# Seven more warming matmuls behind the second product, and a fixed order for the first twelve products

## The chip, the cores and the metric

The kernel runs on one core of a Trainium2 chip. The metric is the device time of one execution in microseconds (us); less is better. The time of a kernel is the median over its runs. The profile is of one execution, and its times count from the first instruction of that execution.

## The reference

The inputs are 2048 tokens of 512 channels. Branch A is attention of 32 heads of 16 channels over a dilated local window (8 keys, every second token back). Branch B is a gated feed-forward layer with 1792 hidden channels. A sigmoid gate per token mixes both. Cut to what matters:

```
def _A_ref(x, wqkv, wo):
    qkv = (x @ wqkv) ...                      # 512 -> 3 * 512: queries, keys, values
    W, dil = 8, 2
    idx = pos[:, None] - (jnp.arange(W) * dil)[None, :]
    logits = where(idx >= 0, sum_d(q * k[idx]) * scale, -1e9)
    o = sum_w(softmax(logits) * v[idx])
    return o @ wo

def _B_ref(x, w_gate, w_up, w_down):
    return (gelu(x @ w_gate) * (x @ w_up)) @ w_down

g = sigmoid((x * gate_w).sum(-1, keepdims=True))
return g * _A_ref(x, ...) + (1 - g) * _B_ref(x, ...)
```

All of it is float32. All matrix products run on TensorE (PE); the local attention runs on VectorE (DVE).

## The kernel before, in words

Tokens are split by parity (even and odd), since the window has a step of two; each parity has 1024 tokens, in 8 tiles of 128 (`jj` from 0 to 7, two blocks `blk` of four tiles, `BT = 4`). The 512 input channels are four chunks `kc` of 128 (`KC = 4`). Every float32 operand is split into a high part in the type fp32r and a low part (the rest): `split` (L82 to L87) rounds on ScalarE (ACT, L86) or with a cast on DVE (L84), and DVE subtracts (L87). A product of two operands is then three matmuls: high by high, low by high, and high by low. In the text, a "product" is one such matmul of 128x128 by 128x512.

The kernel begins with `WARM = 31` matmuls of zeros in bfloat16 (L71, L72), 128x128 by 128x128 each, into a PSUM bank that nothing reads. They depend only on the memset of `warm` (L69). Behind them stand the products of the first stage: the keys and queries of half of the heads for the even tokens. For each chunk `kc` (loop at L795) the weights `WC[0, kc]` are loaded by `load_cb` (L164) and the tokens `X[0, blk, kc]` by the DMAs at L803; both are split. The very first token chunk (`kc = 0`, `blk = 0`) is loaded in two pieces of columns, the first 128 tokens (tile `jj = 0`) and the other 384 (tiles 1 to 3), so that the first products can begin before the second piece is there. The eight tiles accumulate in eight PSUM banks (`ps`, tags `p` and `acc0` to `acc3`; tile 7 has `acc3`), and `qkv_mm` (L185, matmul at L191) issues three products for each tile and chunk: 4 x 8 x 3 = 96 in the stage. In the profile the operands of chunk 0 and 1 show as `g` (weights), `A` (tokens of block 0) and `rt` (tokens of block 1).

Behind the first stage `take_first` (L196) copies the results out (ACT and DVE), then come the values (`project(0, 1)`), and the feed-forward layer `ffn` for the even tokens (products at L480 for gate and up, at L520 for down), into which the remaining projections are put as pieces; then the same for the odd tokens; last the output products (L742). The attention (`scores`, `softmax`, `mix`: long DVE instructions at L288, L291, L326, L330) is dealt out between these steps by `pull`.

The order on each engine isn't that of the text. A planner at build time plays the program through in simulated time and takes, on each engine, the instruction of the highest priority (place in the text, moved back by `BEHIND` for the attention) whose inputs are there at that simulated moment. `paced` (L347) adds an edge that only the planner sees: the instruction isn't planned ahead of the matmul that was recorded last in `LAST`. It costs no wait on the chip; each engine then runs its list in order, held by semaphores where data are needed.

Of the kernel before, what the change touches and what calls it, by code (L numbers as in the profile page):

```python
# [16 lines left out]
P = 128  # L17
# [11 lines left out]
UH = UC // DH  # L29
NU = D // UC  # L30
WARM = 31
BEHIND = 150
PACE = (0.9, 1.12)
LOAD = 4.0
BT = 4
# [9 lines left out]
def tile_gated_mix(ctx: ExitStack, tc: tile.TileContext, xt, wqkv, wff, wo, out):  # L45
    nc = tc.nc
# [17 lines left out]
    def bank(tag):  # L64
        return psum.tile([P, 512], F32, name=tag, bufs=BUFS.get(tag, 1))


    warm = pool.tile([P, P + 96], mybir.dt.bfloat16, name="warm")[:, :P]
    nc.vector.memset(warm, 0.0)  # L69
    idle = bank("p")  # L70
    for _ in range(WARM):  # L71
        nc.tensor.matmul(idle[:, :P], warm, warm, start=True, stop=True)  # L72
    zero = pool.tile([W, UC], F32, name="zero")
    nc.vector.memset(zero, 0.0)

# [23 lines left out]


    X, XOP, XR, WC = {}, {}, {}, {}
    LAST = []

    def fetch_x(par, kc):

# [79 lines left out]
    def qkv_mm(ps, par, jj, cb, kcs, c0=0, cn=512):  # L185
        t = slice((jj % BT) * P, (jj % BT + 1) * P)
        for kc in kcs:
            xh, xl = X[par, jj // BT, kc]
            wh, wl = WC[cb, kc]
            for n, (a, w) in enumerate(((xh, wh), (xl, wh), (xh, wl))):  # L190
                LAST[:] = [nc.tensor.matmul(ps[:, :cn], a[:, t], w[:, c0:c0 + cn], start=(kc == 0 and n == 0),  # L191
                                            stop=(kc == KC - 1 and n == 2))]
# [154 lines left out]
    def paced(ins):  # L347

        tc.add_manual_dep(ins.ins, LAST[-1].ins.name, mybir.DependencyInfo(mybir.DependencyClass.Sync,
                          mybir.DependencyReason.SCHED_ONLY), reason="pace")  # L350
# [39 lines left out]
    def pull(budget, key=None):  # L390
        credit[0] += budget
        while credit[0] > 0 and (key is None or key not in done):
            with tc.high_priority(offset=-BEHIND):
                c = next(fill, None)
# [80 lines left out]
    def product(ps, a, w, start):  # L475
        for kc in range(2):
            ah, al = XOP[a, kc]
            wh, wl = (x[:, kc * P:(kc + 1) * P] for x in w)
            for n, (w_, a_) in enumerate(((wh, ah), (wh, al), (wl, ah))):
                LAST[:] = [nc.tensor.matmul(ps, w_, a_, start=(start and kc == 0 and n == 0),  # L480
                                            stop=(kc == 1 and n == 2), skip_group_check=True)]
# [27 lines left out]
    def down(par, gr, t, b):  # L509
# [6 lines left out]
        for i in range(2):  # L516
            hh_, hl_ = Hs[2 * gr + i, b]
            d = WD[2 * gr + i]
            for n, (a, w) in enumerate(((hh_, d[:, :512]), (hh_, d[:, 512:]), (hl_, d[:, :512]))):
                LAST[:] = [nc.tensor.matmul(pp, a[:, ts], w, start=(i == 0 and n == 0 and gr == 0),  # L520
                                            stop=(i == 1 and n == 2), skip_group_check=True)]
# [216 lines left out]
    def by_unit(pa, oT, u, t, first, last):  # L738
        oh, ol = (x[:, t * P:(t + 1) * P] for x in oT)
        wh, wl = WO[u]  # L740
        for n, (a, b) in enumerate(((oh, wh), (oh, wl), (ol, wh))):
            LAST[:] = [nc.tensor.matmul(pa, a, b, start=(first and n == 0), stop=(last and n == 2),  # L742
                                        skip_group_check=True)]
# [51 lines left out]
    for kc in range(KC):  # L795
# [4 lines left out]
        for blk in range(2):  # L800
# [4 lines left out]
            if not blk:  # L805
                sp()
    ps = [bank(next(names)) for _ in range(NP)]
    for kc in range(KC):
        for jj in range(NP):
            qkv_mm(ps[jj], 0, jj, 0, (kc,))  # L810
    for t in (*KS.values(), *VS.values()):
        for c in range(2):
            paced(nc.gpsimd.dma_start(t[c, :W], zero))
# [79 lines left out]
```

## Time and profile before

| what | value |
|---|---|
| time, median of 3 runs | 616.45 us |
| the three runs | 614.82, 616.45, 616.71 us |
| span of the profiled execution | 614.2 us |
| the profiled execution's own time | not given apart from the span; the median of the runs lies 2.25 us above the span |
| PE busy (matmul) | 604.1 us, 98%, 2839 instructions |
| DVE busy | 513.7 us, 84% |
| ACT busy | 376.9 us, 61% |
| POOL busy | 82.5 us, 13% |
| DMA | 132.48 MB moved, 216 GB/s in the mean |

Line numbers (L191) are those of the kernel before. A line of the timeline gives the start, the time taken, the engine and line, the operation with its output and inputs, the number of instructions merged into it, and in brackets the idle time of the engine before it with what released it. PEld is the load of a matmul's stationary operand, which overlaps the matmuls. The chain of waits is followed back from the last instruction; each of its pieces is what ended last at that moment. A queue name with q behind it (SPq, POOLq) is an engine's issue of DMAs.

### The profile page before, as it was taken

The numbers are of one execution on the slowest core, as the hardware profiler recorded it, in microseconds if no ns is written. First come the engines' busy times: TensorE is split into PE (matmuls) and PEld (weight loads), VectorE is DVE, ScalarE is ACT, GpSimd is POOL, SyncE is SP. The second block draws the span as 40 slices with busy tenths as digits, with TensorE's granted clock in tenths as the row PEclk, the third lists the DMA queues.
The fourth block names the chain that finished last, engine by engine and source line by source line (L and its number), as shares of the span: only waits on it lengthen the run. The fifth ranks groups of instructions, "written<-read, shape, count | busy, mean of one in ns | idle before, by whom it ended". The sixth has DMA issues, their size and how long they took to land.

```text
span 614.2 us, 8246 instructions
## 1 busy us (share of the span) xinstructions
PE 604.1 (98%) x2839; PEld 505.3 (82%) x2839; DVE 513.7 (84%) x598; ACT 376.9 (61%) x633; POOL 82.5 (13%) x110
## 2 busy tenths in 40 slices
PE   9999998999999999999999999999999999999997
PEld 7899886877878888888889888888888888888885
DVE  6849699878998888756698998899899889797972
ACT  6554545674867877857356439447756676685632
POOL 0061011120212121101100002101011101101300
PEclk9999999999999999999999999999999999999999
DMA  8398949797889988995639969787888769937724
GB/s 286 98 252 253 319 145 299 192 262 226 204 225 277 305 210 219 280 231 179 237 93 330 305 174 266 210 235 186 238 200 221 162 225 215 268 86 206 91 64 154
DMA packets 85591, 132.48 MB, mean 216 GB/s; under 512 B 8111, under 2 KB 52271, under 8 KB 85550
## 3 DMA queue, kind: packets, MB, share of 16 engines
q1 hardware_dynamic: 63742, 94.27, 46.9%
q0 software_dynamic: 12672, 32.84, 28.1%
q10 hardware_dynamic: 9136, 4.85, 2.6%
q8 instruction: 22, 0.36, 0.3%
q14 instruction: 19, 0.16, 0.1%
HBM read 67.18 MB, written 36.77 MB: 169 GB/s over the span
## 4 chain that ended last, share of the span: by engine, by line
PE 81%; issue 8%; DMA 7%; DVE 3%; ACT 0%; POOL 0%; SPq 0%; POOLq 0%; DVEq 0%; ACTq 0%
PE p L480 35%; PE acc L191 15%; PE acc L520 11%; PE p L520 11%; PE p L742 5%; PE p L191 4%; DMA raw<-wff 3%; PE acc L742 2%; DMA g<-raw 2%; DMA d<-r 1%; DVE prod L326 1%; DMA raw<-xt 1%; DMA ws<-raw 1%; DVE raw L423 0%; DVE prod L330 0%
## 5 line engine op out<-in xcount | busy, mean ns | idle before, releaser
L480 PE MATMUL p<-S,g 128*128 128x512 f32 x672 | 166.6, 389 | 0.8 <-DVE c L490 0.8
L480 PEld LDWEIGHTS p<-S,g 128*128 128x128 f32 x672 | 126.0, 188 | 27.3 <-DVE c L490 1.3
L480 PE MATMUL p<-A,g 128*128 128x512 f32 x504 | 127.4, 390 | 2.9 <-ACT g L446 1.2
L480 PEld LDWEIGHTS p<-A,g 128*128 128x128 f32 x504 | 94.2, 188 | 23.9 <-DMA g<-raw 1.8
L288 DVE TENSOR_TENSOR prod<-kq 128x2048 f32<-128x2048 f32 x32 | 73.1, 2284 | 13.2 <-DMA kq<-kq 5.9
L326 DVE TENSOR_TENSOR prod<-v,lg 128x2048 f32<-128x2048 f32 x32 | 73.0, 2281 | 6.4 <-DMA v<-vs 4.9
L442 POOL DMA_DIRECT2D g<-raw x42 | 36.4, 867 | 298.3 <-ACT g L441 145.5
L291 DVE TENSOR_REDUCE lg<-prod 128x128 f32<-128x2048 f32 x32 | 73.0, 2282 | 0.3
L520 PE MATMUL p<-d,hh 128*128 128x512 f32 x224 | 68.6, 389 | 0.0
L520 PE MATMUL acc<-d,hh 128*128 128x512 f32 x224 | 60.7, 390 | 1.1 <-DMA d<-r 1.1
L520 PEld LDWEIGHTS acc<-d,hh 128*128 128x128 f32 x224 | 42.0, 188 | 10.4 <-DMA d<-r 1.4
L446 ACT ACTIVATE g<-raw 128x1024 fp32r<-128x1024 f32 (+1 forms) x42 | 41.3, 988 | 13.1 <-PE p L480 12.8
L520 PEld LDWEIGHTS p<-d,hh 128*128 128x128 f32 x224 | 42.0, 188 | 8.8
L490 DVE TENSOR_TENSOR c<-p,s 128x512 f32<-128x512 f32 x56 | 38.2, 685 | 12.9 <-PE p L480 12.6
L441 ACT ACTIVATE g<-raw 128x1024 fp32r<-128x1024 f32 (+1 forms) x42 | 41.3, 983 | 9.9 <-DVE raw L423 9.5
L485 ACT ACTIVATE s<-p 128x512 f32<-128x512 f32 x56 | 33.1, 593 | 21.4 <-PE p L480 21.2
L497 DVE TENSOR_TENSOR hl<-c,hh 128x512 fp32r<-128x512 f32 x56 | 38.0, 679 | 9.3 <-ACT hh L496 9.3
L494 DVE TENSOR_TENSOR c<-c 128x512 f32<-128x512 f32 x56 | 38.3, 685 | 8.4 <-ACT c L586 7.9
L520 PE MATMUL p<-d,hl 128*128 128x512 f32 x112 | 42.9, 389 | 0.0
L496 ACT ACTIVATE hh<-c 128x512 fp32r<-128x512 f32 x56 | 35.1, 626 | 9.7 <-DVE c L494 9.2
L533 ACT ACTIVATE rt<-p 128x512 f32<-128x512 f32 x48 | 27.9, 594 | 20.2 <-PE p L520 20.1
L191 PE MATMUL acc<-g,A 128*128 128x258 f32 (+2 forms) x228 | 39.5, 306 | 0.0
(146 smaller groups left out, 912.1 us busy)
## 6 DMA issues: line engine op xcount, KB each, us to landing
g<-raw POOLq DMA_DIRECT2D x28, 512.0 KB, 7.3
raw<-wff SPq DMA_DIRECT2D x42, 256.0 KB, 3.8
ws<-g SPq DMA_DIRECT2D x14, 768.0 KB, 5.5
g<-ws SPq DMA_DIRECT2D x14, 768.0 KB, 6.6
r<-wff SPq DMA_DIRECT2D x28, 256.0 KB, 4.3
d<-r POOLq DMA_DIRECT2D x28, 256.0 KB, 6.4
g<-raw POOLq DMA_DIRECT2D x14, 384.0 KB, 5.9
v<-vs SPq DMA_DIRECT2D x8, 512.0 KB, 7.7
```

The costliest lines, as they stand in the source:

```text
L191: LAST[:] = [nc.tensor.matmul(ps[:, :cn], a[:, t], w[:, c0:c0 + cn], start=(kc == 0 and n == 0), stop=(kc == KC - 1 and n == 2))]
L288: paced(nc.vector.tensor_tensor(prod, spans(k, jj), q[:, jj:jj + 2, None, :].to_broadcast([P, 2, W, UC]), op=OP.mult))
L291: nc.vector.tensor_reduce(two_of(lg, jj), prod.rearrange("p j w (h d) -> p (j w) h d", d=DH), axis=AX.X, op=OP.add)
L326: paced(nc.vector.tensor_tensor(prod.rearrange("p j w (h d) -> p (j w) h d", d=DH), spans(v, jj).rearrange("p j w (h d) -> p j w h d", d=D ...
L441: nc.scalar.activation(lo, raw, AF.Copy, scale=-1.0)
L446: ins = nc.scalar.activation(hi, raw, AF.Copy)
L480: LAST[:] = [nc.tensor.matmul(ps, w_, a_, start=(start and kc == 0 and n == 0), stop=(kc == 1 and n == 2), skip_group_check=True)]
L490: nc.vector.tensor_tensor(c, ps, s, op=OP.add)
L494: nc.vector.tensor_tensor(ge, ge, up, op=OP.mult)
L497: nc.vector.tensor_tensor(hl_, ge, hh_.bitcast(F32), op=OP.subtract)
L520: LAST[:] = [nc.tensor.matmul(pp, a[:, ts], w, start=(i == 0 and n == 0 and gr == 0), stop=(i == 1 and n == 2), skip_group_check=True)]
L742: LAST[:] = [nc.tensor.matmul(pa, a, b, start=(first and n == 0), stop=(last and n == 2), skip_group_check=True)]
```

## The change

Behind the first two products of tile 0 (high by high, low by high, both on the first 128 tokens) stand `FILLERS = 7` more matmuls of the same zeros as the 31 at the start. They write 128 columns of the bank of tile 7, whose first product later starts the bank anew. Behind them stand the other ten products of chunk 0, block 0, in a written order. All nineteen matmuls are `paced`, each behind the one ahead of it, so the planner can't move them against each other; `LAST` now exists from the 31 on, so that the first of the nineteen has one to stand behind. The general loop leaves out the twelve products that `begin` has issued. The number of products, their operands and their sums are unchanged.

```
+FILLERS = 7
...
+    LAST = []
     for _ in range(WARM):
-        nc.tensor.matmul(idle[:, :P], warm, warm, start=True, stop=True)
+        LAST[:] = [nc.tensor.matmul(idle[:, :P], warm, warm, start=True, stop=True)]
...
-    LAST = []
...
     ps = [bank(next(names)) for _ in range(NP)]
+
+    def begin():
+
+        xh, xl = X[0, 0, 0]
+        wh, wl = WC[0, 0]
+
+        def one(jj, a, w, start):
+            ins = nc.tensor.matmul(ps[jj], a[:, jj * P:(jj + 1) * P], w, start=start, stop=False)
+            paced(ins)
+            LAST[:] = [ins]
+
+        def fillers(n):
+            for _ in range(n):
+                ins = nc.tensor.matmul(ps[-1][:, :P], warm, warm, start=True, stop=True)
+                paced(ins)
+                LAST[:] = [ins]
+
+        one(0, xh, wh, True)
+        one(0, xl, wh, False)
+        fillers(FILLERS)
+        for jj in range(1, BT):
+            one(jj, xh, wh, True)
+        one(0, xh, wl, False)
+        for a, w in ((xl, wh), (xh, wl)):
+            for jj in range(1, BT):
+                one(jj, a, w, False)
+
+    begin()
     for kc in range(KC):
         for jj in range(NP):
-            qkv_mm(ps[jj], 0, jj, 0, (kc,))
+            if kc or jj >= BT:
+                qkv_mm(ps[jj], 0, jj, 0, (kc,))
```

## The prediction, made before the changed kernel was run

> **What bounds the kernel now.** I read the page first: the span, the busy shares and the chain that ended last.
>
> ```profile
> span 614.2 us, 8246 instructions
> ...
> PE 604.1 (98%) x2839; PEld 505.3 (82%) x2839; DVE 513.7 (84%) x598; ACT 376.9 (61%) x633; POOL 82.5 (13%) x110
> ...
> PE 81%; issue 8%; DMA 7%; DVE 3%; ACT 0%; POOL 0%; SPq 0%; POOLq 0%; DVEq 0%; ACTq 0%
> ```
>
> PE is busy for 604.1 of 614.2 us and holds 81% of the chain. So a change on PE counts at full size if it lies on the chain, and only the first 13 us are edited. Next, PE's timeline of that stretch.
>
> ```profile
> 1.00 3.49 PE L72 MATMUL p<-warm 128*128 128x128 bf16 x31 [1.00 <-DVE warm L69]
> 4.32 1.22 PE L191 MATMUL p<-g,A 128*128 128x512 f32 x2
> 5.95 0.80 PE L191 MATMUL p<-g,A 128*128 128x512 f32 x1 [0.41 <-DVE A L84]
> ...
> 8.67 1.76 PE L191 MATMUL acc<-g,A 128*128 128x512 f32 x4
> 10.27 0.62 PE L191 MATMUL p<-g,rt 128*128 128x512 f32 x2
> ```
>
> The 31 warming matmuls run from 1.00, two products follow at 4.32, and then PE waits for the cast of the other 384 tokens: this is where the seven fillers go. Products overlap in this view, so I take their spacing from the chain of waits in order of time.
>
> ```profile
> 1.20 4.31 DMA raw<-xt
> ...
> 5.53 0.37 DVE A L84
> ...
> 5.95 0.80 PE p L191
> 6.75 0.85 PE acc L191 x2
> 7.60 1.28 PE p L191 x3
> 8.88 1.55 PE acc L191 x4
> 10.43 0.46 PE p L191 x2
> 10.90 0.47 PE acc L191 x2
> ...
> 12.28 0.91 PE p L191 x4
> ```
>
> Three products take 1.28 us at 7.60, that is 0.427 us each; four take 0.91 us at 12.28, that is 0.2275 each. The chain passes from the DMA of the tokens over the cast (ready at 5.90) into PE and stays there: the ten slow products between 5.95 and 10.43 are on the path. Why are they slow? By the line's own answer and by the table of stretches:
>
> ```profile
> L191 PE MATMUL p<-g,A x8: 389/632/797, 4.3 to 11.4; 128*128 128x512 f32 x8
> ...
> 7.95:9.95 2.00, 2.00 (x6) 1.54 (x5) 0.98 (x3) 1.34 (x3) 0.00 (x0) 1.00 1.05 406
> 10.27:12.27 2.00, 2.00 (x10) 1.65 (x9) 2.00 (x4) 1.96 (x4) 0.00 (x0) 1.00 1.06 393
> ```
>
> The same shape takes 632 ns early and 389 ns later. In the slow stretch and in the fast one PE is 2.00 us of 2.00 busy and the DMA share is 1.05 and 1.06, so neither a wait nor the DMA load makes the difference; what is left is PE's own clock. The clock column reads 1.00 in both stretches and doesn't show it; the durations do. So PE runs at about half pace until some 10.1 us, within the last of the four products that begin at 8.88.
>
> **The change, part by part.** The fillers: the 31 warming matmuls take from 1.00 to 4.32, or 3.32 / 31 = 0.107 us each at the slow pace, so seven take 0.75 us. The two products occupy PE from 4.32 to 4.32 + 2 x 0.427 = 5.17, and the third begins at 5.95: a hole of 0.78 us (the 0.41 in the bracket counts only from the modelled end of the second). The fillers fit with 0.03 us to spare. Their cost is nothing while the second token piece lands as it did; if it came 0.75 us sooner, they would hold the third product up by all of 0.75. They carry no semaphore of another engine: their operand is the memset that the 31 already waited for, and their bank is next written by PE itself.
>
> The order: the trace before already runs two products of tile 0, then tiles 1, 2 and 3, then three in `p`, then four in `acc`, and the written order has the same five products first and the same operands ahead of each place after that. What each place waits for:
>
> ```profile
> 5.81 0.68 DVE L87 TENSOR_TENSOR g<-c,g 128x512 fp32r<-128x512 f32 x1
> 6.41 0.55 DVE L87 TENSOR_TENSOR A<-raw,A 128x384 fp32r<-128x384 f32 x1
> ...
> 7.52 0.69 DVE L87 TENSOR_TENSOR rt<-raw,rt 128x512 fp32r<-128x512 f32 x1
> ...
> 8.57 0.63 ACT L86 ACTIVATE A<-raw 128x512 fp32r<-128x512 f32 x1 [1.08 <-DMA raw<-xt]
> ```
>
> The low weights are there at 6.49, the low tokens of block 0 at 6.96, block 1's low part at 8.21, chunk 1's high part at 9.20. The order by itself costs and saves nothing.
>
> The gain is what a filled hole does to the clock. PE's work would be unbroken from 1.00 on. What the rows say of the rise: a stretch unbroken from 1.00 to 5.17 (4.17 us) showed no rise, one from 5.95 to about 10.1 (4.2 us) ended in one. So the length alone doesn't settle it, and I bound the new moment of the rise from both sides: 5.95 or earlier, or 10.1 as now.
> - At 5.95 or earlier the ten products end at 5.95 + 9 x 0.2275 + 0.39 = 8.39 instead of 10.43: 2.04 us saved. The inputs allow it but for about 0.1 us: the seventh product wants the low tokens of 6.96 and would begin at 7.3; the four behind the twelve end near 9.3, and chunk 1's high part is there at 9.20.
> - At 10.1: nothing saved, or, with the fillers exposed, up to 0.75 lost.
> - Halfway, at 8.0: five products slow and five fast, the last ending at 9.4, 1.05 saved.
>
> Which value? The nearest measurement is the three times. The fastest run, 614.82, lies 1.63 and 1.89 us under the other two, nearly the 2.04 of the upper bound. I read it (a reading, nothing shows it) as a run in which the clock rose ahead of the wait, and the other two as runs like the profiled one. With the hole filled, most runs should be like the fastest. I take the mean, 1.76, rounded to 1.75 us.
>
> The Trainium skill, page "TensorE: Matmul & The Clock Gate", section "Part 1: The HAM clock gate", says that the array starts at half clock and is let up to full clock at the end of a 3.4 us window of sustained work, with windows that run free of the kernel's start. The trace agrees with two paces in a ratio of 0.427 to 0.2275; counted back from a rise near 10.1, windows would end near 6.7 and 3.3, the hole lies within the one that ends at 6.7, and by that page the filled hole would move the rise to 6.7, three products slow at most, an estimate of 1.65 us saved.
>
> Does a saving at 10 us reach the end? The first stage ends earlier and its readers are waiting already; then the chain:
>
> ```profile
> ACT kq L815 <- PE p L191: 3.9, 1, 3.9
> DVE kq L202 <- PE p L191: 1.5, 1, 1.5
> ...
> 42.95 10.11 PE acc L191 x84
> ...
> 53.08 4.02 DMA ws<-raw
> ...
> 57.18 9.04 DMA raw<-wff
> ...
> 66.28 20.70 issue
> ...
> 91.23 5.05 DMA d<-r
> ```
>
> ACT waits 3.9 and DVE 1.5 us for PE at the end of the first stage, more than the 1.75 for ACT and nearly as much for DVE, so both can follow. PE is on the chain without a break from 5.95 to 53.06; the DMAs after that are issued behind it, up to the next waits of PE:
>
> ```profile
> PE p L480 <- ACT g L446: 1.2, 1, 1.2
> PE acc L520 <- DMA d<-r: 1.1, 1, 1.1
> ...
> 86.99 0.85 POOL L442 DMA_DIRECT2D g<-raw  x1 [30.28 <-PE p L480]
> ```
>
> The POOL transfer ahead of those waits was itself let go by PE after 30.28 us, so it moves with PE. I carry the whole saving: against the profiled span 614.2 - 1.75 = 612.45 us, and with the 2.25 us by which the median stands above the span, 614.7 us.
>
> **Rivals.**
>
> The clock doesn't move, or the lead is lost. The rise stays near 10.1, because the fillers aren't enough work or because the 4.17 us without a rise show that something else decides; or DVE, 84% busy, holds the feed-forward weights back at the waits of 1.2 and 1.1 us. For it: that stretch, and the 1.5 us of DVE's slack. Against it: the chain runs through PE. Time 616.45, up to 617.2 with the fillers exposed. Chance 0.07.
>
> The median run has little to gain. If runs like 614.82 are common, a new median of before lies there, and the change moves the two kernels together. For it: one run of three. Against it: two of three. The time is again near 614.8, while the kernel before reads lower than 616.45. The same section of the skill speaks for it, against the change: it says that one kernel meets 6, 11 or 14 cold matmuls by where the window lies at its start. Chance 0.05.
>
> Slower: the planner deals the later work out differently. Nineteen matmuls are now planned as a chain and seven are new, so simulated moments after the first stage may shift, and near ties fall the other way. The place would be the weight sums on DVE:
>
> ```profile
> 87.94 0.42 DVE L423 TENSOR_TENSOR raw<-raw 128x256 f32<-128x256 f32 x1
> 88.28 2.28 DVE L291 TENSOR_REDUCE lg<-prod 128x128 f32<-128x2048 f32 x1
> ```
>
> A sum of 0.42 us stands just ahead of an attention step of 2.28. If they change places, ACT's and POOL's steps and the 5.05 us DMA of the chain come 2.28 later. One such turn costs 2.28 - 1.75 = 0.5 net; from two turns on it is slower by more than 0.3%: 616.45 + 4.56 - 1.75 = 619.3 us. Against it: after the twelfth product the trace runs block 1 and chunk 1 in groups of two and four rather than three by tile, so the planner's PE was waiting for splits there and can take up 0.75 us unseen. Chance 0.18.
>
> **How the numbers follow.** About 0.3%, or 1.85 us, is what a measurement of this kernel can tell from no change. The bounds are 614.6 and 618.3. My forecast, 614.7 us, has 0.70; its own range is 614.0 (all 2.04 saved, and some scatter of the fastest run) to 615.6 (a rise halfway). The bound for faster falls within it, so I give 0.45 of it to faster and 0.25 to within 0.3%. The first two rivals, 0.12, are within 0.3%; the third, 0.18, is slower. Sum: faster 0.45, same 0.37, slower 0.18. The range is 614.0 to 617.2, which takes in the first two rivals and the exposed fillers, and leaves out the slower one.
>
> **What would show it.** In the changed profile: seven 128x128 matmuls between 5.17 and 5.95; no idle time of PE ahead of the third product; at most three products of 632 ns behind it; the first stage's end about 1.75 us earlier; PE's waits near 92 and 96 us no longer than before; the same groups of products on PE from 13 us on. Ten products still at 632 ns, or an earlier stage and longer waits of PE later, would make the forecast wrong, each in its own step.

## The result, and the profile after

The changed kernel took 613.21 us in the median of 14 runs (612.31 to 614.50); the kernel before, in 14 runs, 615.18 us (613.17 to 616.71). The medians differ by 1.97 us and the means (615.11 and 613.29) by 1.82. The ratio is 0.9973, with a 95% interval of 0.9961 to 0.9986: the interval lies wholly below 1, and the ratio is at the edge of the 0.3% that the prediction set as its bound. In all means below, three single runs above 630 us are left out (646.82 and 753.48 of the kernel before, 1233.41 of the written order without fillers). The profiled execution has a span of 611.2 us and a time of its own of 613.01; it stands 1.81 us above its span.

The lines of the page that answer to those of before:

```profile
span 611.2 us, 8260 instructions
...
PE 603.0 (99%) x2846; PEld 504.5 (83%) x2846; DVE 513.8 (84%) x598; ACT 376.5 (62%) x633; POOL 82.4 (13%) x110
...
PE 84%; issue 8%; DMA 4%; DVE 3%; ACT 0%; POOL 0%; SPq 0%; POOLq 0%; DVEq 0%; ACTq 0%
```

PE has seven matmuls more and is busy for 1.1 us less. PE's timeline of the start (L74 are the 31 warming matmuls, L822 the fillers, L816 the twelve products):

```profile
1.00 3.49 PE L74 MATMUL p<-warm 128*128 128x128 bf16 x31 [1.00 <-DVE warm L70]
4.33 1.22 PE L816 MATMUL p<-g,A 128*128 128x512 f32 x2
5.36 0.97 PE L822 MATMUL acc<-warm 128*128 128x128 bf16 x7
6.08 0.58 PE L816 MATMUL p<-g,A 128*128 128x512 f32 x1
6.50 0.62 PE L816 MATMUL acc<-g,A 128*128 128x512 f32 x2
...
8.56 0.61 PE L192 MATMUL p<-g,rt 128*128 128x512 f32 x2
```

There is no bracket ahead of the third product any more: PE doesn't wait. It begins 0.13 us later than before (6.08 against 5.95), but two products now take 0.62 us from 6.50 on, where they took 1.06 at 6.54 before; block 1 begins at 8.56, not 10.27. The clock had risen near 6.4 us: the third product starts 0.42 us ahead of the fourth (6.08 and 6.50), the fourth 0.22 ahead of the fifth. The chain of waits shows it too: from the memset of `warm` on it stays on PE over the whole stretch.

```profile
1.00 3.49 PE p L74 x31
4.49 1.06 PE p L816 x2
5.55 0.77 PE acc L822 x7
6.33 0.34 PE p L816
```

Further on, the waits of PE (what waited, on whom, in total, how often, the longest):

```profile
PE p L481 <- DVE c L491: 1.1, 2, 0.6
PE acc L521 <- DMA d<-r: 1.1, 1, 1.1
PE p L74 <- DVE warm L70: 1.0, 1, 1.0
PE p L481 <- DMA g<-raw: 0.8, 2, 0.4
PE p L481 <- ACT g L447: 0.4, 1, 0.4
```

The wait on ACT shrank from 1.2 to 0.4, those on DVE from 1.6 to 1.1. So the trace gained 3.0 us of span, not 1.75: 1.74 by the end of the first stage and the rest at later waits.

The planner's order had also moved at places that the change doesn't touch. On the DMA queue of SP, the first load of `v` (L272) had stood ahead of a store of `ws` and the two weight loads of the third step, and now stood behind them; on ACT the split of a weight block (L441) had moved ahead of a copy (L555) and a store. On PE one product of the second chunk (block 1) had moved from the 32nd to the 44th place. This was a second possible cause, and several of the experiments are about it.

### The profile page after: what moved, and what is told of

It is laid out like the page before. It is cut to its first block, busy times and chain, and to the rows that moved or that the text cites. A ratio compares the mean times of both kernels' runs of the same rounds, so it can differ in the third digit from the quotient of the medians.

```text
span 611.2 us, 8260 instructions
## 1 busy us (share of the span) xinstructions
PE 603.0 (99%) x2846; PEld 504.5 (83%) x2846; DVE 513.8 (84%) x598; ACT 376.5 (62%) x633; POOL 82.4 (13%) x110
## 4 chain that ended last, share of the span: by engine, by line
PE 84%; issue 8%; DMA 4%; DVE 3%; ACT 0%; POOL 0%; SPq 0%; POOLq 0%; DVEq 0%; ACTq 0%
PE p L481 35%; PE acc L192 16%; PE acc L521 11%; PE p L521 11%; PE p L743 5%; PE p L192 3%; PE acc L743 2%; DMA g<-raw 2%; DMA raw<-wff 1%; DMA d<-r 1%; DVE prod L327 1%; PE p L74 1%; DVE raw L424 0%; DVE prod L331 0%; PE p L816 0%
## 5 line engine op out<-in xcount | busy, mean ns | idle before, releaser
L331 DVE TENSOR_TENSOR prod<-prod 128x1024 f32<-128x1024 f32 x32 | 39.0, 1220 | 0.4
```

Source lines behind the costliest of these rows:

```text
L331: nc.vector.tensor_tensor(prod[:, :, :4], prod[:, :, :4], prod[:, :, 4:], op=OP.add)
```

## The experiments

Two theories: the clock (the hole behind the second product kept PE's clock low in most runs, and the fillers close it), and the later order (the moved `v` load and split save time, and the fillers are beside the point). A third, that the written order of the twelve products helps by itself, is tested on the way.

**Only the written order.**

```
-FILLERS = 7
+FILLERS = 0
```

> The written order of the first twelve products without any filler; on ACT, DVE, POOL and the DMA queue the later order is that of the kernel before. If the clock of PE is the cause (the hole between 5.2 and 6.0 us keeps the clock low): as before, mean near 615.1 us, runs scattered over some 3 us. If the written order by itself is the cause: near 613.3 us, as after. If the later order of the DMA queue is the cause: as before, 615.1, since that order is the old one here.

Mean of 11 runs 615.85 us (614.02 to 618.82), against 615.44 for 34 runs of before on the same chip; ratio 1.0011 (0.9993 to 1.0028). The written order by itself brings nothing that can be measured.

**The later order without fillers**, run twice. The marks are the instructions named above; the moved product on PE isn't among them, and stays where the kernel before has it.

```
-FILLERS = 7
+FILLERS = 0
...
+    behind(("v0", 0, 0), ("fetch", 2))          # first load of v behind the third step's weights
+    behind(("v1", 0, 0), ("v0", 0, 0))
+    behind(("copy", 0, 0), ("lo", 0, 1, 1))     # copy of p behind the split of g
+    behind(("vals", 0, 7, 1), ("copy", 0, 0))
```

> No fillers, but the later order of after on the DMA queue (the first load of v behind the store of ws and the weights of the third step) and on ACT (the split of g ahead of the copy of p), held by planner edges. If the clock alone is the cause: as before, 615.1 us in the mean. If the later order alone is: 613.3. If both have a part: the wait of PE near 92 us shrinks from 1.2 to about 0.4 and the mean is about 0.8 us under that of the kernel before, 614.3, with the old scatter of 3 us.

> The second kernel once more (no fillers, later order of after): its twelve runs gave 614.64 us in the mean against 615.44 of before, but its trace stands within 0.2 us of before up to the wait near 92 us. If the later order is worth nothing: mean 615.4 here. If it is worth 0.8: 614.6 again.

The first time 614.64 us in the mean of 12 against 615.44 for before; the second time 615.07 against 614.79 (35 runs of before, another chip). The intervals of both ratios, 0.9988 (0.9971 to 1.0006) and 1.0001 (0.9983 to 1.0018), take in 1. The wait on ACT near 92 us, which the later order was to shrink, is there in both profiles:

```profile
93.12 1.67 PE L482 MATMUL p<-A,g 128*128 128x512 f32 x6 [1.25 <-ACT g L447]
```

That is the first; the second profile, of a run in which the clock rose early, says:

```profile
1.00 3.19 PE L74 MATMUL p<-warm 128*128 128x128 bf16 x31 [1.00 <-DVE warm L70]
4.40 0.73 PE L817 MATMUL p<-g,A 128*128 128x512 f32 x2 [0.21 <-ACT g L88]
5.84 0.50 PE L817 MATMUL p<-g,A 128*128 128x512 f32 x1 [0.72 <-DVE A L86]
...
91.44 1.66 PE L482 MATMUL p<-A,g 128*128 128x512 f32 x6 [1.28 <-ACT g L447]
```

Here the first two products take 0.73 us and not 1.22: without any filler, the clock was up before the first product, and a hole of 0.72 us behind the second didn't bring it down again. That the faster runs of the kernel before are of this kind is a reading: none of them was profiled. These twelve times stand in two groups, seven from 613.2 to 614.2 and five from 615.8 to 618.6; the twelve of the first time (613.3 to 616.8) have no such gap.

**The fillers with the later order of before.**

```
+    behind(("keep", 1), ("v0", 0, 0))           # ws store behind the load of v, as before
+    behind(("lo", 0, 1, 1), ("vals", 0, 7, 1))  # split of g behind the store, as before
```

> The seven fillers and the written order, but the later order of the DMA queue and of ACT held as in the kernel before. If the clock alone is the cause: 613.3 us in the mean, scatter 2 us or less. If the later order alone is: 615.1. If both have a part: about 614.1, PE's wait near 92 us back at about 1.2, and the narrow scatter of after.

Mean 613.85 us of 12 runs (611.84 to 615.42), 1.59 under before; ratio 0.9975 (0.9961 to 0.9990). PE's start and the place near 92 us:

```profile
4.46 1.22 PE L817 MATMUL p<-g,A 128*128 128x512 f32 x2
5.49 0.97 PE L823 MATMUL acc<-warm 128*128 128x128 bf16 x7
6.22 0.77 PE L817 MATMUL p<-g,A 128*128 128x512 f32 x1
6.79 0.66 PE L817 MATMUL acc<-g,A 128*128 128x512 f32 x2
...
90.70 1.65 PE L482 MATMUL p<-A,g 128*128 128x512 f32 x6
93.77 0.50 PE L522 MATMUL acc<-d,hh 128*128 128x512 f32 x1 [1.10 <-DMA d<-r]
```

With the old later order the gain is there in full, and the wait near 92 us has gone altogether. The theory of the later order falls: it is not needed for the gain, and without fillers it brings none that can be measured.

**The changed kernel again**, on two further chips.

> The changed kernel unchanged, on the same chip as the other three, so that they can be compared with it: 613.3 us in the mean by every theory, runs from 612.3 to 614.5.

> The changed kernel once more beside the kernel before, for the size of the effect, which differed between the first comparison (1.8 us in the mean) and the second (1.1). If the effect is the removal of the runs in which the clock rises late: no run above some 615.5, a mean 0.8 to 1.8 us under that of before, and before's runs in two groups. If it is a fixed saving: the fastest runs of both differ as much as the means.

614.36 us in the mean of 12 against 615.44 (ratio 0.9981, 0.9962 to 1.0000), and 613.54 against 614.96 for 28 runs (0.9978, 0.9962 to 0.9995). The first mean is 1.1 us above the 613.3 expected, and four of its twelve runs lie above 614.5, one at 617.03; of the second twelve, one (615.60) is just above 615.5. So three comparisons give 1.8, 1.1 and 1.4 us in the means. In the first of these profiles the clock was up before the first product, and the seven fillers, at the fast pace, took 0.56 us and left a hole that did no harm:

```profile
4.41 0.73 PE L816 MATMUL p<-g,A 128*128 128x512 f32 x2 [0.26 <-ACT g L88]
4.98 0.56 PE L822 MATMUL acc<-warm 128*128 128x128 bf16 x7
6.19 0.50 PE L816 MATMUL p<-g,A 128*128 128x512 f32 x1 [0.65 <-DVE A L86]
```

**The seven at the start.** The kernel before, with no other edit; the planner then moved the `v` load, the split and the product on PE as in the changed kernel:

```
-WARM = 31
+WARM = 38
```

> The kernel before with 38 warming matmuls at the start instead of 31: the seven stand ahead of the first product, not behind the second, and the twelve products keep the planner's own order. If what counts is that PE has no hole before the third product: the first product begins near 5.1 us, the third where it did, the clock is up at 7.9 us at the latest, the twelfth product begins near 8.6 and not 9.9, and the mean is that of after, about 613.9. If the place behind the second product matters: as before, 615.4, or worse by the delay of the first two.

The first product begins at 4.99 and the third at 6.18, the clock is up before the third, and the twelfth begins at 8.51:

```profile
1.00 4.24 PE L72 MATMUL p<-warm 128*128 128x128 bf16 x38 [1.00 <-DVE warm L69]
4.99 0.92 PE L191 MATMUL p<-g,A 128*128 128x512 f32 x2
6.18 0.51 PE L191 MATMUL p<-g,A 128*128 128x512 f32 x1 [0.26 <-DVE A L84]
```

So the clock and the start are as after. In the times no gain shows: 614.47 in the mean of 12 against 614.79, ratio 1.0000 (0.9987 to 1.0012). On this chip 22 of 35 runs of before were under 614.9 us, so there was less to gain; yet four fillers gained 0.8 us on the same chip (below), and why this kernel's time didn't follow its start stays open. As far as these runs go, a start like that of after isn't by itself enough for the gain in time.

**The hole moved.** 24 warming matmuls and the seven fillers, 31 in all:

```
-WARM = 31
+WARM = 24
```

> 24 warming matmuls at the start and the seven behind the second product: 31 in all as before, and the hole now lies ahead of the first product (from 3.6 to 4.3 us). If any hole in the first 6 us holds the clock down: the clock rises in the profile between 7.7 and 11.2 us, and the mean is about 615.0. If the hole ahead of the third product is the one that counts: as after, about 613.9, with a rise before 7.9 us.

615.77 us in the mean of 12, ratio 1.0015 (1.0002 to 1.0028): slower than before, and only one run under 614.9. The profile has the hole ahead of the first product, none behind the second, and slow products up to about 10 us:

```profile
4.43 1.22 PE L816 MATMUL p<-g,A 128*128 128x512 f32 x2 [0.69 <-ACT g L88]
5.45 0.97 PE L822 MATMUL acc<-warm 128*128 128x128 bf16 x7
6.18 0.78 PE L816 MATMUL p<-g,A 128*128 128x512 f32 x1
6.75 1.05 PE L816 MATMUL acc<-g,A 128*128 128x512 f32 x2
...
10.28 0.62 PE L192 MATMUL p<-g,rt 128*128 128x512 f32 x2
```

The order on all engines and the number of fillers are as after; only the seven warming matmuls at the start are missing, so that the hole lies in another place, and the gain is gone. So neither the moved instructions nor the fillers as such bring it. As this kernel has 31 matmuls of zeros, like the kernel before, it doesn't tell the place of a hole from the number of these matmuls. That it is slower than before fits the clock theory: a run escapes the hole only if the clock rises ahead of it, the earliest rise in any profile is near 3.65 us, and this hole begins at 3.53 where that of before begins at 5.34.

**Four fillers.**

```
-FILLERS = 7
+FILLERS = 4
```

> Four fillers instead of seven: 0.43 us of the hole of 0.78 is filled, 0.35 stays. If the hole must be closed whole: as before, rise in the profile after 9 us, mean near 615.2. If a short idle time is tolerated: as after, rise before 7.9 us, mean about 613.9. In between if the effect is in proportion: about 614.5.

613.96 us in the mean of 11 (612.99 to 614.65), ratio 0.9986 (0.9976 to 0.9997). The twelfth product begins at 8.41. Four gained 0.8 us; seven were not run on this chip, and gained 1.1 to 1.8 on others. How much of the hole may stay open it doesn't tell: in this profile the spacing of the fillers falls from 0.12 to 0.06 us (starts at 5.49, 5.61, 5.70 and 5.76), so the clock rose while they ran, and the 0.26 us left ahead of the third product at 6.07 came after the rise.

**Fourteen fillers.**

```
-FILLERS = 7
+FILLERS = 14
```

> Fourteen fillers: 14 x 0.107 = 1.50 us at the slow pace against a hole of 0.78. If the clock is still low there, the third product begins at 6.7 instead of 6.0; if it has risen, 14 fillers take about 0.8 and cost nothing. The clock rises by 7.9 us either way. Mean between 613.9 and 614.7 by the clock theory; the planner's order of the second chunk moves too, so the time is read with care. By the prediction's step (an uncovered filler costs its whole time) 614.7.

614.16 us in the mean of 10 (613.50 to 615.04), ratio 0.9989 (0.9974 to 1.0003). In its profile the clock was up early, fourteen fillers took 0.96 us, and the third product began at 6.21, so the cost at the slow pace wasn't seen; the mean stands between the two values expected and doesn't decide between them.

**One warming matmul and no filler.**

```
-WARM = 31
+WARM = 1
...
-FILLERS = 7
+FILLERS = 0
```

> One warming matmul and no filler: PE's work begins at about 4.3 us, with the hole after the second product. If the clock rises after one whole window of work that begins behind the hole: rise between 9.4 and 12.8 us in the profile, never before, nine or more slow products, mean 615.8 to 616.5. If the 31 already bought nothing whenever the hole is open, it is as the kernel before in the mean, 615.1.

618.75 us in the mean of 10 (616.49 to 621.25), ratio 1.0068 (1.0048 to 1.0089). Slower than either expectation, but part of it is later: the planner's order changed in many places, and the profile loses another 2 us after 126 us. At the start, products are slow up to about 10.6 us.

The starts of four products on PE in all profiles (us; counted in order on PE, warming ones left out), worked out from the traces:

| kernel | 3rd | 12th | 96th | 501st | span |
|---|---|---|---|---|---|
| before | 5.95 | 9.95 | 29.12 | 103.49 | 614.2 |
| written order, no filler | 5.94 | 9.94 | 29.05 | 103.66 | 617.0 |
| later order, no filler, first | 6.17 | 9.88 | 28.93 | 103.36 | 614.3 |
| later order, no filler, again | 5.84 | 8.18 | 27.22 | 101.69 | 612.1 |
| hole moved | 6.18 | 10.05 | 29.10 | 103.52 | 614.1 |
| one warming matmul | 5.82 | 9.82 | 29.26 | 103.00 | 616.9 |
| after | 6.08 | 8.34 | 27.38 | 100.90 | 611.2 |
| fillers, later order of before | 6.22 | 8.67 | 27.71 | 100.93 | 612.3 |
| after, again | 6.19 | 8.53 | 27.57 | 101.12 | 612.1 |
| after, third | 5.76 | 8.06 | 27.54 | 101.23 | 610.9 |
| 38 at the start | 6.18 | 8.51 | 27.56 | 100.95 | 612.2 |
| four fillers | 6.07 | 8.41 | 27.54 | 101.22 | 612.6 |
| fourteen | 6.21 | 8.36 | 27.40 | 101.15 | 613.0 |

All seven profiles with the hole filled have the twelfth product between 8.06 and 8.67. Of the six with a hole, five have it between 9.82 and 10.05 and one at 8.18. In that of the written order the hole, of 0.39 us by the bracket, lies ahead of the first product, since the weights came later.

A line at 614.9 us, drawn after the runs, parts the profiled runs of known time alike: the eight in which the clock rose early lie under it (612.70 to 614.75), the four in which it rose late above it (615.83 to 618.82). Counted over all runs, 70 of 83 with the hole filled were under 614.9 us, and 56 of 111 of the kernel before.

## Why the prediction was right or wrong

**The time was missed.** It said 614.7, with a range from 614.0, and 613.21 came. The step that failed is the base: the prediction laid its saving on 616.45, the median of three runs, and added 2.25 us above the profiled span. The median of 14 runs of the same kernel is 615.18, and the changed kernel's profiled execution stands 1.81 above its span (613.01 to 611.2). Of the 1.49 us by which 614.7 was too high, 1.27 are the base and 0.22 the saving. The second rival had named the reason, that runs like 614.82 may be common, and gave it 0.05: six of the 14 runs, and 56 of 111 in all, were under 614.9. Its own time, 614.8, missed too, since it put the saving at nothing. The range should have held the base as one of its unknowns: the three times alone span 1.9 us.

**The saving was right in size, in part by luck.** 1.75 predicted, 1.97 measured in the medians, 1.82 in the means, 1.1 and 1.4 in two repeats. In the trace the first stage's end is 1.74 us earlier (96th product, 27.38 against 29.12), within the bound of 2.04. But that is what a late run gains, and only eight of the 14 runs of before were above 614.9: 8/14 of 1.75 would be 1.0 in the mean. The rest came from gains further on that the prediction didn't have (below).

**The clock step was right.** The traces show it: in five of six profiles with a hole in the first 6 us the slow pace lasts to about 10 us, in the sixth the clock was up before the hole, and with the hole filled, ahead of the first product or behind the second, the rise comes by about 6.8 us in all seven. The reading of 614.82 as a run in which the clock rose ahead of the wait is made likely by the second profile of the later order, but not shown for that run.

Most of the gain is the removal of the late runs, but not all of it. Under 614.9, the changed kernel's runs are faster too: 613.29 against 613.81 us in the mean in the first comparison, 613.65 against 614.13 and 613.35 against 613.88 in the repeats, some 0.5 us each. An estimate from the same line: in the first comparison eight of 14 runs late at 2.28 us each (616.09 against 613.81) give 1.3, and 0.5 more make the 1.8 measured. The expectation that a pure removal leaves the fastest runs level holds on the last chip (612.65 and 612.58), not in the first comparison (613.17 and 612.31).

The rule of the Trainium skill, page "TensorE: Matmul & The Clock Gate", section "Part 1: The HAM clock gate" (windows that run free of the kernel's start), agrees with the scatter of the rise, from about 3.7 to about 6.8 us over the seven profiles of filled kernels. That the rise ends a 3.4 us window of sustained work isn't borne out in full: in three profiles it came 2.7 to 2.9 us after the first matmul. The estimate of 6.7 for the profiled run of before can't be tested, since another execution need not lie the same in the windows; its saving of 1.65 us belongs to two slow products, and three would give 1.44 (2.04 less 0.2 for each).

**The fillers' cost** of nothing was wrong in size, since the hole was: the prediction counted 0.427 us for each of the two products, but in the trace of before the second starts 0.59 behind the first (4.32 and 4.91), so the hole from 5.34 to 5.95 is 0.61 us, not 0.78. After, seven fillers took 0.72 (5.36 to 6.08). The cast that the third product waits for was done at 5.67 in this execution, where it was done at 5.90 in that of before:

```profile
5.31 0.36 DVE L86 CAST A<-raw 128x384 fp32r<-128x384 f32 x1 [1.38 <-DMA raw<-xt]
```

So the third product began 0.13 us later than before, though its data were there 0.2 us sooner: the fillers held it up by some 0.35 us in this execution.

**The later order.** "The same groups of products on PE from 13 us on" was wrong: the planner moved one product of the second chunk on PE and two instructions further on, as the third rival had it, though at other places than the one named. The latter two have no cost or gain that the runs can tell from zero: 0.8 us less and 0.3 more without fillers, 0.5 more with them. Nor does the written order keep every place of the old one: one product stands 10th and not 8th, which cost nothing that can be measured (the written order by itself, above).

**Carried through whole** was short: the profiled span fell by 3.0, not 1.75. At the 501st product the lead had grown from 1.74 to 2.59 us, where PE's wait on ACT shrank from 1.19 to 0.35. The row ahead of it on DVE, before and then after:

```profile
74.68 2.29 DVE L288 TENSOR_TENSOR prod<-kq 128x2048 f32<-128x2048 f32 x1 [2.85 <-DMA kq<-qs]
```

```profile
72.09 2.29 DVE L289 TENSOR_TENSOR prod<-kq 128x2048 f32<-128x2048 f32 x1 [2.01 <-DMA kq<-qs]
```

The load of `kq` landed 2.6 us earlier with a lead of 1.74, and the split of the weights, which stands behind these DVE steps, came with it. All seven filled profiles show such a second gain (0.6 to 1.2 us by the table); the one early clock without fillers doesn't (its lead of 1.90 at the 96th product is 1.80 at the 501st). The fillers need not be its cause: the seven also share the moved product on PE, which the early clock without fillers lacks; the moved hole has that order without the gain, and the kernel with one warming matmul, whose order changed in many places, gains 0.6 between the same products. Why the transfers ahead of it ran quicker stays open. From the 501st product to the end the profiles take from 509.7 us (after, third) to 513.9 (one warming matmul), 510.7 before and 510.3 after, with no sign of the fillers in it. So 3.0 us is the distance of one late rise from one early one with 0.4 us of such scatter on top, and the medians, in which half of the runs of before are early ones too, are the measure.

## What to carry to other kernels

Where PE bounds a kernel, look at the first 10 us by the duration of equal matmuls, not by the clock column: a short wait between the warming matmuls and the first dense stretch went here with some 4 us more of slow pace, worth 1.7 us by the end of the first stage, and a few matmuls of zeros in it took that away. More of them ahead of it did so in the trace, but no gain in time was seen. Such a gain is mostly one in the share of late runs: take the base from many runs, and put its scatter into the range. Count a hole from the starts of the instructions around it, not from a spacing taken elsewhere. And compare the order on every engine after a small edit, then hold it fixed and test it by itself before the edit gets the credit.

## What the runs showed of the hardware that was not expected

In three profiles (after, again; later order, again; fourteen fillers) the spacing of the warming matmuls themselves falls from 0.107 to 0.056 us, at 3.65 to 3.9 us, 2.7 to 2.9 us after the first of them, while the clock column reads 1.00. PE had run nothing but matmuls of zeros by then, so these are enough for the rise.

Once the clock is up, a wait of 0.72 us behind the second product doesn't bring it down (later order, again), nor does one of 0.61 ahead of the first (fourteen fillers). A wait of 0.41 by the same bracket (before), or of 0.69 ahead of the first product (hole moved), that comes before the rise goes with a rise near 10 us.

The first product behind matmuls of zeros or behind a wait takes longer until the next one starts than the later ones do: 0.59 us at 4.32 and again at 5.95, against 0.43, at the slow pace (before); 0.34 against 0.23 at the fast one (after, again, at 6.19).
